# A one-core kernel of sparse attention and a gated feed-forward: keys of units 3 to 5 copied ahead of the first value gathers, and one weight piece loaded from another queue

## The chip, the core and the metric

One NeuronCore of one Trainium2 chip runs the whole program: TensorE (PE) for matmuls and transposes, VectorE (DVE), ScalarE (ACT), GpSimd (POOL) and SyncE (SP), with 16 DMA engines that serve the queues of SP, ACT and POOL. The metric is the device time of one launch in microseconds (us).

## What is computed

Block-sparse attention over 4 batches, 8 heads, 768 positions of width 64, then a feed-forward layer on the result. Cut to what matters:

```python
scores = scale * np.matmul(q, k.transpose(0, 1, 3, 2))
# kept: the diagonal block and its neighbours, the first and last block rows and columns,
# and three sampled key blocks for each block of queries (blocks of 32 positions)
attn = softmax(np.where(mask, scores, -1e9))
x = np.matmul(attn, v)              # laid out as 3072 tokens of 512
h = x @ w_in                        # 512 x 2048
sp = np.maximum(h, 0.0) + np.log1p(np.exp(-np.abs(h)))
out = (h * erf(sp)) @ w_out         # 2048 x 512
```

The two weights arrive as 64-bit floats, so each is 8.4 MB.

## The kernel before

**Units.** A batch has 24 blocks of 32 queries. The 22 inner blocks are worked on two at a time: unit n of a batch is blocks 1+2n and 2+2n, so there are 11 "m" units, and four "f" units more for the first and last block, which look at every key. For an m unit `scores` multiplies the queries (`qm`) with neighbouring keys, with the first and last block, and with the sampled keys; `soft_max`, `soft_exp` and `soft_turn` make probabilities (`less`, `pf`, and `pT`, the transposed and split copy); `values` multiplies them with the values into `po`; `norm` divides (`rinv`, `xf`); `turn` writes the transposed result to `xT`, from which the feed-forward starts. Four units make one chunk of `xT`.

**Sampled keys and values.** Which blocks are sampled is known only at run time. `gather` has POOL copy six key blocks for a unit from `kx` to two of the six buffers `kg` (three units' worth). Values go through a table in device memory: `split_v` scales and splits them (`vn`), SP stores `vn` to `vtab` (four stores), and `gather_v` fills one of six buffers `vbuf` per query block: one or two loads by SP (neighbours, and the first and last block) and one indirect DMA by POOL (the sampled blocks). `gathers(most)` first issues all key copies that have a free `kg`, then up to `most` value gathers that have a free `vbuf`.

**Weights.** `load_w` brings the weights in pieces: the first weight ("i") in eight pieces of 1 MB on SP, the second ("o") in six of 1 MB (named here wo0, wo2, to wo10 by their first row block, loaded by ACT's queue) and in pieces 12 to 15 of 0.5 MB each, which land in buffers `raw` that belong to other stages at other times. `decode` turns a pair of 64-bit rows into 32-bit floats in three DVE steps: `room<-wo`, `room<-wo,room`, `wo<-wo,room`. The loads wo0 to wo6 overwrite places of w_in pieces that must be decoded first, and wo8 and wo10 the places of wo4 and wo6. `weights()` runs the decode, the squares for a scale (`sq`), the 16-bit high and low halves and the correction `rest`; `ratios()` needs all of them, and the first gate of the feed-forward needs `ratios()`.

**Order.** SP and POOL issue in the order of the program. PE, ACT and DVE are put in order by the compiler up to the fourth group of the feed-forward, and from there in the order of the program too. The engines run their rows strictly in order. The warm-up is the loop over `begun` from 0 to 5 (`FIRST`): for each unit `values` of the unit two before it, its scores and softmax, then `gathers()`, then three steps of `weights()`. All later work is the loop over the groups of the feed-forward, one unit in most steps.

**Waits in rows of the program order.** DMAHW0 to DMAHW7 are eight semaphores that the DMAs of SP and ACT take in turn; a DMA also waits until the one that had its semaphore before has landed. DMASW are those of POOL's DMAs.

Of the kernel before, what the change touches and what calls it, by code (L numbers as in the profile page):

```python
# [31 lines left out]
def sparse_attention_moe(ctx: ExitStack, tc: tile.TileContext, qT, kT, v, sampled, w_in, w_out, out):  # L32
# [39 lines left out]
    KGS, VGS = 6, 6  # L72
# [90 lines left out]
    def order_q(b, u):  # L163
        t, half = divmod(u, 2)
        qt = qts[b, t][:, :, half * 2 * BLOCK : (half + 1) * 2 * BLOCK].rearrange("p r (j c) -> p r j c", c=BLOCK)
        for a in range(2):
            place = qms[half][a * D : (a + 1) * D, :, :, a, :]
            if b == 0 and 0 < u <= FIRST:
                act.activation(place, qt[a * D : (a + 1) * D], AF.Copy, scale=D**-0.5)
            else:  # L170
                dve.tensor_scalar(place, qt[a * D : (a + 1) * D], D**-0.5, None, ALU.mult)
# [219 lines left out]
    def load_w(key, i):  # L391

        if key == "o" and i >= 12:
            tag, bufs = (("vraw", 1), ("xT", 3), ("xT", 3), ("x", 2))[i - 12]
            rows = w_out[i * P : (i + 1) * P].bitcast(I32)
            if tag == "x":
                parts = [mo.tile([P, 512], I32, tag=tag, name=f"raw_{i}_{u}", bufs=bufs) for u in range(2)]
            elif tag == "vraw":
                parts = [ld.tile([P, H // 2, KT * D], I32, tag=tag, name=f"raw_{i}", bufs=bufs).rearrange("p a b -> p (a b)")[:, :1024]]
            else:  # L400
                parts = [mo.tile([P, 1024], I32, tag=tag, name=f"raw_{i}", bufs=bufs)]
            c = 0
            for raw in parts:
                (sp if i == 15 else act).dma_start(raw, rows[:, c : c + raw.shape[1]])
                c += raw.shape[1]
            places[key, i] = parts
            return
        if key == "i":
            raw = slots(wi, 1 + 2 * i, 4) if i < 8 else slots(wo, 2 * i - 16, 4)
            part, kt = divmod(i // 2, NK)  # L410
            sp.dma_start(raw, w_in[kt * P : (kt + 1) * P, part * 1024 : (part + 1) * 1024].bitcast(I32))
        else:
            raw = slots(wo, 2 + 2 * i if i < 8 else 10 + 2 * (i - 8), 4)
            rows = w_out[i * P : (i + 2) * P, :].bitcast(I32).rearrange("(n p) c -> p n c", n=2)
            act.dma_start(raw.rearrange("p (n c) -> p n c", n=2), rows)
        places[key, i] = [raw]
# [254 lines left out]
    def norm(b, u, part):  # L671
        po = pos.pop((b, u, part))
        tag = f"{b}_{u}_{part}"
        gr = slice(0, 4) if part is None else slice(2 * part, 2 * part + 2)
        n = gr.stop - gr.start
        rinv = st.tile([P, 4], F32, tag="rinv", name=f"rinv_{tag}")[:, :n]
        dve.tensor_scalar(rinv, po[:, gr, D], EPS * 2.0**P_SHIFT, None, ALU.add)
        dve.reciprocal(rinv, rinv)
        if not part:
            xfs[b, u] = at.tile([P, 4, D], F32, tag="xf", name=f"xf_{b}_{u}", bufs=1)  # L680
        dve.tensor_tensor(xfs[b, u][:, gr], po[:, gr, :D], rinv.unsqueeze(2).to_broadcast([P, n, D]), ALU.mult)
# [115 lines left out]
    units = []  # L797
# [9 lines left out]
    def gathers(most=VGS):  # L807

        nonlocal kfree, vfree
        while kjobs and kfree >= 2 and kjobs[0][0] in have_k:  # L810
            kfree -= 2
            gather(*kjobs.pop(0))
        while vjobs and vfree and most and vjobs[0][0] in have_v:
            gather_v(*vjobs.pop(0))
            vfree -= 1
            most -= 1
# [46 lines left out]
    def seen(unit):  # L863

        if unit[0] == "m":
            return unit[1], unit[2], None
        if unit[2] % 2 == 1:
            return unit[1], NU, unit[2] // 2
        return None
# [6 lines left out]
    def used_values(place):  # L876
        nonlocal vfree
        if place[2] is None:
            vfree += 2
        elif place[2] == 1:  # L880
            vfree += 3
# [19 lines left out]
    for i in range(0, 16, 2):  # L901
        if i in (0, 2, 6):
            load_q(0, 1 + (i + 1) // 3)
        if i:
            load_w("i", i)
    load_w("o", 15)
    order_q(0, 0)
    have_k.add(0)
    ixgen = indices()
    next(ixgen)  # L910
    gathers()
    with tc.high_priority():
        max_v(0, 0)
        max_v(0, 1)
# [5 lines left out]
            for half in range(2):  # L920
                split_v(0, quad, half)
    have_v.add(0)
    for i in (13, 12, 14):
        load_w("o", i)
    for begun in range(FIRST):
        with tc.high_priority():
            if begun >= 2:
                place = seen(units[begun - 2])
                values(*place)
                used_values(place)  # L930
                norm(*place)
                turn(*place, True)
            unit = units[begun]
            scores(unit)
            used_keys(unit)
            soft_max(unit)
            next_queries(begun)
            soft_exp(unit, True)
            soft_turn(unit)
        gathers()  # L940
        later(3)
        if 0 < begun < B:
            zero_rows(begun)
        if begun < 4:
            behind(begun)
# [106 lines left out]
```

## Time and profile before

| | us |
|---|---|
| median of 3 runs | 788.03 (783.29 to 788.62) |
| the profiled execution | 781.89 |
| its span on the core | 780.1 |
| PE busy | 716.6 (92%) |
| ACT busy | 597.8 (77%) |
| DVE busy | 556.1 (71%) |
| POOL busy | 201.4 (26%) |

The page's second part cuts the span into 40 slices of 19.5 us. PE is 2 to 7 tenths busy in the first four and 8 or 9 in all but the last. DMA is at 9 tenths in the first three slices. All that follows concerns the first 130 us; rows of the trace give the start of a group of instructions, its duration, its engine, the line (L48 is a helper that issues every operation, so tiles tell them apart), the operation, and in brackets the idle time just before it and what ended it. "SPq", "ACTq" are the queues' own DMA issues.

### The profile page before, as it was taken

How to read it: one execution, taken by the hardware profiler on the slowest of the kernel's cores; microseconds unless marked ns; L12 is line 12 of the kernel's file. 1: busy time of each engine (PE TensorE's matmuls, PEld its weight loads, DVE VectorE, ACT ScalarE, POOL GpSimd, SP SyncE). 2: the span in 40 equal slices, each digit the busy share in tenths (PEclk: the TensorE clock that was granted, in tenths of full speed). 3: DMA queues.
4: the chain of work that ended last, by engine and by line, in shares of the span. 5: the costliest groups of instructions: out<-in, count | busy, mean ns of one | idle time of the engine just before them, and what ended most of it. 6: DMA issues, size and time to landing. Idle time of an engine off the chain costs nothing.

```text
span 780.1 us, 26222 instructions
## 1 busy us (share of the span) xinstructions
PE 716.6 (92%) x11136; PEld 501.0 (64%) x11136; DVE 556.1 (71%) x1043; ACT 597.8 (77%) x1035; POOL 201.4 (26%) x397
## 2 busy tenths in 40 slices
PE   2447788999899999999999999999999999999997
PEld 1334546766577777666677776666767676666663
DVE  7795998887677777767766777757867766564553
ACT  3656799888768878888788777878778877787774
POOL 2247531314343312032423312033433120000000
PEclk9668999999999999999999999999999999999999
DMA  9999765997799986836989989828977676231000
GB/s 311 410 253 303 211 140 121 186 240 163 162 210 168 220 196 171 205 97 146 195 175 186 171 191 206 204 59 176 218 150 176 130 148 144 53 51 28 8 28 27
DMA packets 188053, 129.45 MB, mean 166 GB/s; under 512 B 137760, under 2 KB 160928, under 8 KB 186912
## 3 DMA queue, kind: packets, MB, share of 16 engines
q1 hardware_dynamic: 173440, 83.98, 51.7%
q10 hardware_dynamic: 8608, 25.96, 10.6%
q0 software_dynamic: 5888, 17.84, 9.7%
q8 instruction: 87, 1.43, 0.8%
q14 instruction: 30, 0.25, 0.1%
HBM read 82.81 MB, written 12.95 MB: 123 GB/s over the span
## 4 chain that ended last, share of the span: by engine, by line
PE 80%; DVE 7%; DMA 6%; ACT 3%; issue 2%; SPq 1%; ACTq 1%
PE h L48 31%; PE o L48 30%; PE s_m L48 9%; PE po_None L48 5%; PE s_f L48 2%; DMA qt<-in_qT_dram 2%; DMA wo<-in_w_out_dram 2%; DVE room L48 2%; PE po L48 1%; DVE wo L48 1%; ACT x L48 1%; DMA vbuf<-in_v_dram 1%; DMA pT_f<-p_f 1%; PE rest L48 1%; SPq L48 1%
## 5 line engine op out<-in xcount | busy, mean ns | idle before, releaser
L48 PE MATMUL h<-xT,wi 128*128 128x256 f16 x2304 | 272.1, 275 | 6.4 <-DVE y L48 4.5
L48 PE MATMUL o<-wo,g 128*128 128x512 f16 x1152 | 264.5, 379 | 0.3 <-DVE g L48 0.2
L48 PEld LDWEIGHTS <-wi 128*128 128x128 f16 x2304 | 223.6, 99 | 47.1 <-issue 4.8
L48 ACT ACTIVATE x<-x 128x512 f32<-128x512 f32 x288 | 181.3, 630 | 8.9
L48 PEld LDWEIGHTS <-g 128*128 128x128 f16 x1152 | 109.6, 98 | 120.4 <-DVE g L48 1.3
L48 POOL DMA_INDIRECT vbuf<-vtab,idx x88 | 103.5, 1176 | 250.2 <-PE po_None L48 170.6
L48 DVE SCALAR_TENSOR_TENSOR y<-y,x 128x512 f32<-128x512 f32 x96 | 66.2, 689 | 78.5 <-ACT x L48 78.5
L48 PE MATMUL s_m<-kx,qm 128*64 128x64 f32 (+1 forms) x1408 | 95.7, 247 | 26.6 <-DVE qm L48 14.3
L48 ACT ACTIVATE x<-h,isg 128x512 f32<-128x512 f32 x96 | 65.4, 681 | 69.0 <-PE h L48 67.3
L48 PEld LDWEIGHTS s_m<-kx,qm 128*64 128x64 f32 x1408 | 70.8, 145 | 36.2 <-ACT sq_i L48 14.3
L48 POOL COPY kg<-kx 128x128 f32 x264 | 79.7, 349 | 51.9 <-PE s_m L48 34.0
L48 ACT ACTIVATE y<-y 128x512 f32<-128x512 f32 x96 | 59.6, 621 | 35.2 <-DVE y L48 26.0
L48 DVE TENSOR_REDUCE less_m<-s_m 128x4 f32<-128x1024 f32 x44 | 53.7, 1221 | 35.2 <-PE s_m L48 35.2
L48 DVE SCALAR_TENSOR_TENSOR g<-y,sums,g 128x512 f16<-128x512 f32 x96 | 72.5, 756 | 3.4
L48 ACT ACTIVATE pf_m<-s_m,less_m 128x256 f32<-128x256 f32 x176 | 68.5, 472 | 4.6 <-PE turned L48 2.3
L48 PE MATMUL s_m<-kg,qm 128*64 128x96 f32 x704 | 65.4, 258 | 1.9 <-POOL kg L48 1.9
L48 DVE SCALAR_TENSOR_TENSOR y<-y,h 128x512 f32<-128x512 f32 x96 | 65.4, 681 | 0.7
L48 ACT ACTIVATE y<-x 128x512 f32<-128x512 f32 x96 | 60.4, 629 | 2.9
L48 PEld LDWEIGHTS <-pT_m 128*32 128x32 f16 x4224 | 38.6, 94 | 24.8 <-issue 20.1
L48 DVE TENSOR_SCALAR g<-y,sums 128x512 f16<-128x512 f32 x96 | 48.3, 504 | 3.4
L48 PE MATMUL po_None<-vbuf,pT_m 128*32 128x65 f16 (+1 forms) x4224 | 44.8, 196 | 3.9 <-ACT pf_m L48 2.9
L48 PEld LDWEIGHTS s_m<-kg,qm 128*64 128x64 f32 x704 | 45.2, 146 | 3.7 <-POOL kg L48 2.3
(106 smaller groups left out, 608.5 us busy)
## 6 DMA issues: line engine op xcount, KB each, us to landing
vbuf<-vtab SPq DMA_DIRECT2D x80, 195.0 KB
vraw<-in_v_dram ACTq DMA_DIRECT2D x9, 768.0 KB
vtab<-vn SPq DMA_DIRECT2D x16, 390.0 KB
vbuf<-vtab SPq DMA_DIRECT2D x12, 520.0 KB
wo<-in_w_out_dram ACTq DMA_DIRECT2D x6, 1024.0 KB
qt<-in_qT_dram SPq DMA_DIRECT2D x20, 256.0 KB
kr<-in_kT_dram ACTq DMA_DIRECT2D x12, 384.0 KB
vbuf<-vtab SPq DMA_DIRECT2D x32, 130.0 KB
```

The lines of the kernel that those rows point to most:

```text
L48: done = call(*args, **kwargs)
```

## The change

Piece 13 of the second weight is issued by SP right behind piece 15, where ACT issued it before, ahead of pieces 12 and 14. The first two units' calls of `gathers` now copy keys only (`gathers(0)`), and value gathers begin after unit 2; so POOL copies the keys of units 3, 4 and 5 before the first six value gathers. `values` of unit 0 moves from ahead of unit 2's scores to behind that round of gathers.

```diff
-                (sp if i == 15 else act).dma_start(raw, rows[:, c : c + raw.shape[1]])
+                (sp if i in (13, 15) else act).dma_start(raw, rows[:, c : c + raw.shape[1]])
...
     load_w("o", 15)
+    load_w("o", 13)
...
-    gathers()
+    gathers(0)
...
-    for i in (13, 12, 14):
+    for i in (12, 14):
         load_w("o", i)
     for begun in range(FIRST):
         with tc.high_priority():
-            if begun >= 2:
+            if begun >= 3:
                 place = seen(units[begun - 2])
                 values(*place)
...
-        gathers()
+        gathers(VGS if begun >= 2 else 0)
+        if begun == 2:
+            with tc.high_priority():
+                place = seen(units[0])
+                values(*place)
+                used_values(place)
+                norm(*place)
+                turn(*place, True)
```

The compiler's order moves with it. **Place 1.** ACT, early in the program, before: `raw_303` is piece 13, `qm` the scaled queries, `pf_m_0` the exponentials of unit 0.

```order
L48 ACTIVATE sq_i_401,sums<-wi 128x1024 [waits DMAHW2_49,DVE_49]
L48 ACTIVATE qm_111<-qt_0_133 64x8x32 [waits DMAHW6_49]
L48 ACTIVATE qm_111<-qt_0_133 64x8x32
L48 DMA raw_303<-in_w_out_dram 128x1024 [waits DMAHW0_49]
L48 ACTIVATE qm_110<-qt_1_146 64x8x32 [waits DMAHW4_49,DVE_49,PE_49]
L48 ACTIVATE qm_110<-qt_1_146 64x8x32 [waits DVE_49]
L48 ACTIVATE pf_m_0_338<-s_m_0_309,less_m_0_334 128x256 [waits DVE_49]
```

The same place of the changed program:

```order
L48 ACTIVATE sq_i_382,sums<-wi 128x1024 [waits DMAHW2_49,DVE_49]
L48 ACTIVATE qm_111<-qt_0_133 64x8x32 [waits DMAHW6_49]
L48 ACTIVATE qm_111<-qt_0_133 64x8x32
L48 ACTIVATE qm_110<-qt_1_146 64x8x32 [waits DMAHW4_49,DVE_49,PE_49]
L48 ACTIVATE qm_110<-qt_1_146 64x8x32 [waits DVE_49]
L48 ACTIVATE pf_m_0_338<-s_m_0_309,less_m_0_334 128x256 [waits DVE_49]
L48 ACTIVATE pf_m_0_338<-s_m_0_309,less_m_0_334 128x256 x3
L48 ACTIVATE pT_m_0_343<-turned 128x2x256 [waits PE_49,Activation_49]
```

The DMA that waited for DMAHW0 no longer stands between the queries of units 1 and 2; on SP it stands behind piece 15 and ahead of the first store to `vtab`.

**Place 2.** POOL, before, between the keys of unit 3 (`kg_8`) and those of unit 4 (`kg_9`, `kg_10`):

```order
L48 COPY kg_8_375<-kx_135 128x128 [waits PE_49,Pool_49]
...
L48 DMA vbuf_104<-vtab_115,idx 96x1040 [waits DMAHW2_49,DMAHW1_49,DMAHW3_49,DMASW1_49,DMAHW5_49,DMASW0_49,DVE_49]
L48 DMA vbuf_105<-vtab_115,idx 96x1040
...
L48 DMA vbuf_109<-vtab_115,idx 96x1040
...
L48 COPY kg_9_475<-kx_135 128x128 [waits PE_49,Pool_49]
...
L48 COPY kg_10_479<-kx_135 128x128 [waits PE_49,Pool_49]
```

and in the changed program, from the same row on:

```order
L48 COPY kg_8_375<-kx_135 128x128 [waits PE_49,Pool_49]
...
L48 COPY kg_9_456<-kx_135 128x128 [waits PE_49,Pool_49]
...
L48 COPY kg_10_460<-kx_135 128x128 [waits PE_49,Pool_49]
...
L48 COPY kg_11_562<-kx_135 128x128 [waits PE_49,Pool_49]
...
L48 COPY kg_12_566<-kx_135 128x128 [waits PE_49,Pool_49]
...
L48 DMA vbuf_104<-vtab_115,idx 96x1040 [waits DMAHW2_49,DMAHW1_49,DMAHW3_49,DMASW1_49,DMAHW5_49,DMASW0_49,DVE_49]
```

Twelve copies (two units) moved ahead of the six gathers, which wait for the stores to `vtab`.

**Place 3.** DVE, before, from the first decode step of wo4 (it waits for DMAHW4) to that of wo6 (DMAHW6), `rinv_1` being the norm of unit 1:

```order
L48 TENSOR_SCALAR room<-wo 128x1024 [waits DMAHW4_49]
L48 SCALAR_TENSOR_TENSOR room<-wo,room 128x1024 [waits DVE_49]
L48 TENSOR_SCALAR rinv_1_None<-po_1_None 128x4 [waits PE_49]
L48 SCALAR_TENSOR_TENSOR wo<-wo,room 128x1024 [waits DVE_49]
L48 RECIPROCAL rinv_1_None<-rinv_1_None 128x4 [waits DVE_49]
L48 TENSOR_SCALAR sums<-allm_wi_736 128x1 [waits PE_49]
L48 TENSOR_SCALAR room<-wo 128x1024 [waits DMAHW6_49]
```

and in the changed program, wo4 by DMAHW6 and wo6 by DMAHW7:

```order
L48 TENSOR_SCALAR room<-wo 128x1024 [waits DMAHW6_49]
L48 TENSOR_SCALAR rinv_1_None<-po_1_None 128x4 [waits PE_49]
L48 TENSOR_REDUCE less_m_5_1384<-s_m_5_1359 128x4 [waits PE_49]
L48 TENSOR_SCALAR qm_111<-qt_3_152 64x8x32 x2
L48 SCALAR_TENSOR_TENSOR room<-wo,room 128x1024 [waits DVE_49]
L48 RECIPROCAL rinv_1_None<-rinv_1_None 128x4 [waits DVE_49]
L48 TENSOR_SCALAR sums<-allm_wi_732 128x1 [waits PE_49]
L48 TENSOR_SCALAR room<-wo 128x1024 [waits DMAHW7_49]
L48 SCALAR_TENSOR_TENSOR wo<-wo,room 128x1024 [waits DVE_49]
```

The last decode step of wo4, which frees the place of wo8, now stands behind the row that waits for wo6, and its second step behind the norm of unit 1 and the maximum of unit 5.

## Rows read from the trace of the kernel before

**Rows 1.** Windows: us, busy us (x instructions) per engine, granted clock, DMA share, GB/s.

```profile
86.00:128.00 42.00, 32.95 (x516) 22.64 (x517) 38.83 (x91) 38.39 (x72) 12.20 (x22) 0.92 0.59 136
128.00:200.00 72.00, 72.00 (x1185) 50.27 (x1184) 57.28 (x107) 62.26 (x107) 16.46 (x31) 0.98 0.86 181
200.00:780.00 580.00, 569.02 (x8792) 396.82 (x8790) 394.65 (x715) 448.68 (x764) 131.09 (x264) 1.00 0.69 144
```

**Rows 2.** Windows again, same columns, cut where the DMA load changes.

```profile
45.00:53.25 8.25, 3.82 (x50) 3.67 (x50) 8.25 (x11) 5.09 (x11) 3.89 (x1) 0.71 0.68 182
53.25:90.00 36.75, 26.69 (x488) 16.69 (x490) 25.89 (x49) 24.43 (x51) 28.32 (x47) 0.83 1.03 308
90.00:96.00 6.00, 6.00 (x108) 4.28 (x106) 6.00 (x13) 4.94 (x9) 0.51 (x1) 0.96 0.03 10
```

**Rows 3.** Timeline of DVE: its waits for softmax, weight pieces and queries.

```profile
28.02 0.69 DVE L48 SCALAR_TENSOR_TENSOR pT_m<-turned,pT_m 128x512 f16<-128x512 f32 x1 [3.70 <-ACT pT_m L48]
...
57.23 0.69 DVE L48 TENSOR_SCALAR room<-wo 128x1024 int32<-128x1024 int32 x1 [1.28 <-DMA wo<-in_w_out_dram]
...
64.75 0.75 DVE L48 TENSOR_SCALAR room<-wo 128x1024 int32<-128x1024 int32 x1 [4.30 <-DMA wo<-in_w_out_dram]
...
71.98 0.90 DVE L48 TENSOR_SCALAR room<-wo 128x1024 int32<-128x1024 int32 x1 [2.10 <-DMA wo<-in_w_out_dram]
...
74.46 1.21 DVE L48 SCALAR_TENSOR_TENSOR wo<-wo,room 128x1024 int32<-128x1024 int32 x1
...
78.40 0.69 DVE L48 TENSOR_SCALAR room<-wo 128x1024 int32<-128x1024 int32 x1 [1.39 <-DMA wo<-in_w_out_dram]
...
86.07 0.73 DVE L48 TENSOR_SCALAR room<-wo 128x1024 int32<-128x1024 int32 x1 [1.02 <-DMA wo<-in_w_out_dram]
...
101.06 0.59 DVE L48 TENSOR_SCALAR qm<-qt 64x256 f32<-64x256 f32 x2 [0.75 <-DMA qt<-in_qT_dram]
```

**Rows 4.** Timeline of ACT: piece 13, what follows it, and loads of wo.

```profile
24.27 0.38 ACTq L48 DMA_DIRECT2D raw<-in_w_out_dram  x1
24.78 0.85 ACT L48 ACTIVATE qm<-qt 64x256 f32<-64x256 f32 x2 [9.87 <-DVE i_v L48]
...
50.53 0.41 ACTq L48 DMA_DIRECT2D wo<-in_w_out_dram  x1
...
59.74 1.48 ACT L48 ACTIVATE wi<-wi,sums 128x512 f16<-128x512 f32 x2 [2.75 <-DMA vbuf<-vtab]
...
76.86 0.38 ACTq L48 DMA_DIRECT2D wo<-in_w_out_dram  x1
```

**Rows 5.** Chain that ended last, in order of time: start, us, what.

```profile
14.16 10.09 DMA qt<-in_qT_dram
24.27 0.38 ACTq L48
24.78 0.42 ACT qm L48
```

**Rows 6.** Timeline of POOL: key copies and the first value gather.

```profile
17.55 1.48 POOL L48 COPY kg<-kx 128x128 f32 x6 [0.69 <-issue]
...
20.84 3.98 POOL L48 COPY kg<-kx 128x128 f32 x6 [0.38 <-PE allm_v L48]
49.13 3.89 POOL L48 DMA_INDIRECT vbuf<-vtab,idx  x1 [24.31 <-DMA vtab<-vn]
...
61.24 1.47 POOL L48 COPY kg<-kx 128x128 f32 x6
```

**Rows 7.** Timeline of PE: scores of unit 4, values of units 0 and 1.

```profile
62.05 0.38 PE L48 MATMUL s_m<-kg,qm 128*64 128x96 f32 x2 [1.87 <-POOL kg L48]
...
67.40 0.95 PE L48 MATMUL po_None<-vbuf,pT_m 128*32 128x65 f16 x95
...
70.79 0.96 PE L48 MATMUL po_None<-vbuf,pT_m 128*32 128x65 f16 x96
```

**Rows 8.** Timeline of SP's DMA issues: piece 15, stores to vtab, value loads.

```profile
20.92 2.95 SPq L48 DMA_DIRECT2D raw<-in_w_out_dram  x2
31.71 9.33 SPq L48 DMA_DIRECT2D vtab<-vn  x4
48.42 47.52 SPq L48 DMA_DIRECT2D vbuf<-vtab  x21
```

## The prediction

> **What bounds the kernel now.** I read the windows first, then the waits of each engine in the first 130 us, then the program's order. From 128 us on PE is the bound: busy 72.00 of 72.00 us up to 200, 569.02 of 580.00 after [rows 1]. The change touches nothing there, because the rows from the fourth feed-forward group on keep the order of the program; so its worth is the time by which that stretch begins earlier or later. Before it, PE is not the bound. In 86 to 128 us DVE is busy 38.83 of 42.00 us and ACT 38.39 [rows 1], with the decode of the last weight pieces, their halves and the softmax of units 3 to 7, all of it ahead of the first gate. What starts that stretch is the landing of wo8 at 86.07 [rows 3]. And what sets that landing is the DMA stage ahead of it: from 53.25 to 90 us the DMA engines are loaded 1.03 with 308 GB/s, and in the same time DVE stands five times waiting for a piece of wo, at 57.23, 64.75, 71.98, 78.40 and 86.07, 10.1 us in all [rows 2, 3]. So the question is whether wo8 lands earlier.
>
> Just ahead of that stage there is a gap: from 45 to 53.25 us the DMA moves only 182 GB/s [rows 2]. Nothing is queued: wo0 is issued at 50.53 [rows 4], since its place must be decoded first, and DVE, busy 8.25 of 8.25 us there [rows 2], gets to it no sooner.
>
> **Part 1, piece 13 leaves ACT's queue (place 1).** Its DMA waits for DMAHW0, on which queries landed at 14.16 + 10.09 = 24.25 [rows 5]; it is issued at 24.27, and ACT has by then been idle 9.87 us, from 14.9 [rows 4]. (The idle row names DVE; the chain names the transfer, and the next row of ACT waits only for queries and a free buffer.) Behind it stand the queries of unit 2, the exponentials of unit 0, then its transposes; DVE, free at 24.32, waits 3.70 us for the second half of that work, to 28.02 [rows 3]. Without the DMA ACT can go on at about 20, when unit 0's maximum is there, and DVE has no wait at 24.32, if the weight piece it decodes next has landed; that piece was queued ahead of the queries that landed at 24.25 [rows 5], so it has. DVE's stream up to the decode that frees wo0 is busy, so it moves by the whole 3.7 us, and wo0 is issued at about 47 where it was 50.53.
>
> What is that worth at the DMA? The gap is short of the stage's rate by (308 - 182) x 8.25 = 1.04 MB, or 3.4 us at 308 GB/s [rows 2]. That is the upper bound. The lower is nothing: the value gathers cannot start before the stores to `vtab` have landed (48.42 [rows 8]), and those are bytes that queue behind all of w_in as before. The loads come 3.5 us earlier in a gap of 8.25, so I take half: **-1.7 us** (0 to -3.4).
>
> The piece on SP costs SP nothing that is wanted: it waits there for the same landing, to 24.25, and SP's next row is a store to `vtab`, issued at 31.71 [rows 8], 28 if DVE is 3.7 earlier. Its 0.5 MB now lie ahead of the stores in SP's own queue and no longer in ACT's; all must be moved ahead of the gathers either way, so 0. If they did delay the stores it would be 0.5 MB / 308 GB/s = 1.7 us on the gathers.
>
> The Trainium skill ("DMA: Bandwidth & Descriptors", "Issuing engines are not separate DMA queues") says that all queues end in the same 16 DMA engines and that issuing from another one saves only the issuing engine's time. By that rule the move is worth the 0.38 us of the issue. The rows agree on the bytes, but not on the size of what the issuing engine loses: 9.87 us of waiting.
>
> **Part 2, keys ahead of gathers (place 2).** Six copies take 1.47 us [rows 6]. Before, POOL stood 24.31 us waiting for `vtab` with unit 4's copies behind it, and copied them at 61.24; PE, at the scores of unit 4, waited 1.87 us for them, and the values of unit 0 stood behind those scores, running at 67.40 [rows 6, 7]. Now both units' copies lie in POOL's idle time (12 copies, 2.9 us, or 8.0 by the slowest row, 3.98 for six, where POOL has 24.31 idle [rows 6]); they wait for the scores of units 1 and 2, which PE has done by then. So the scores, the maximum and the exponentials of unit 4 move out of the way, and the values of unit 0 can run when their gathers land. I estimate 65, from 67.40. But all of this lies beside the DMA stage: DVE's rows for it fill its 10.1 us of waits. Worth on the path: 0.
>
> The copies now run beside DVE. In the row of 3.98 us they were slowed to 0.66 us each, against 0.25 for the row of 1.48 [rows 6]. It was POOL that waited, and POOL has time; cost 0. The Trainium skill ("SBUF — State Buffer", "SBUF: two separate sides") says that GpSimd and a DVE instruction with two inputs in that memory exclude each other for a whole instruction, whichever comes first. If DVE always lost, 12 copies of 0.25 would cost it up to 3 us; nothing in the rows shows DVE losing.
>
> **Part 3, what the compiler's order does to wo8 (place 3).** Before, the last decode step of wo4 ran at 74.46, its place was free at 75.67, and wo8 was issued at 76.86, before wo6 landed at 78.40; so ACT's queue went from wo6 to wo8 without a break and wo8 landed 86.07 - 78.40 = 7.67 us after wo6 [rows 3, 4]. Now that step stands behind the row that waits for wo6: 0.69 + 1.21 us after its landing [rows 3] the place is free, and wo8 can be issued 2.0 us after wo6 landed. From then it starts on an empty queue. The nearest row is wo0, which did so: issued 50.53 [rows 4], landed 57.23 [rows 3], 6.7 us. So wo8 lands 8.7 us after wo6 and not 7.67: **+1.0 us**. Bounds: 1.05 MB at the full 308 GB/s is 3.4 us, so 5.4 after wo6 (-2.3); or as slow as before, 7.67, so 9.7 (+2.0).
>
> **Part 4, after wo8.** DVE's wait of 0.75 us at 101.06 is for queries that SP issues behind the value loads of unit 6, which wait for the values of unit 3 [rows 3, 8]. The rows that these values need stand a little nearer to wo8 in DVE's new order, so I take the wait as gone: **-0.75** (0 to -0.75).
>
> **Sum:** -1.7 + 1.0 - 0.75 = -1.45 us. Against the profiled execution's own 781.89 that gives 780.4. The timed runs lie higher, 783.29 to 788.62 with a mean of 786.6 and a median of 788.03, so as a median of runs I say 786.6 - 1.45, near **785**.
>
> **Rivals.** *Nothing gained.* The gap at 45 to 53 is not filled because the gathers come late by what wo0 comes early, and wo8 keeps its distance to 128 us: 786.6. For it: the stage is bound by bytes, and no byte is saved. Against: in the gap the load was 0.68 [rows 2].
>
> *More gained.* The whole gap is filled (-3.4) and, the gathers being through, wo8 moves alone (-2.3, and -0.75): -6.5 us, 780. For it: DMA load falls to 0.03 at 90 us [rows 2], so a queue does empty. Against: both bounds would have to hold at once.
>
> *Slower: DVE's order ties the weights to the values.* The second decode step of wo4 now stands behind the norm of unit 1 and the maximum of unit 5 (place 3), that is behind PE's values of unit 1. These ended at 71.75 and wo4 landed at 71.98 [rows 7, 3], a tie. If they are later than wo4, wo4, wo8 and all behind it are late by the difference. Price: if piece 13 and piece 14 (issued earlier by ACT now) delay the stores, 2 x 1.7 = 3.4, and with +1.0 from part 3 it is +4.4, or 791. It decides as soon as the values of unit 1 end after wo4's landing. For it: values wait for gathers, gathers for stores. Against: the values of unit 0 lose their wait behind unit 4's scores.
>
> **How the numbers follow.** Chances: forecast 0.5, nothing gained 0.2, more gained 0.15, slower 0.15. A measurement of this kernel can tell about 1% (7.9 us) from no change; each case's centre is within that, and only scatter of the runs, some 3 us either way, and cases beyond their bounds carry it out: faster by over 1% 0.1, slower 0.06, within 0.84. The range is 780 (all that can be gained) to 791 (the slower rival).
>
> **What would show it.** Right: no idle of 9.87 us on ACT; DVE's pT step at 24.3; wo0 issued near 47; key copies of units 4 and 5 before 48; wo8 issued about 2 us after wo6 lands and landing near 85; PE's steady stretch from about 126.5. Wrong: `vtab` landing well after 50, values of unit 1 after 73, or wo0 still issued near 50.

## The result, and the profile after

The changed kernel is slower by about one per cent: a median of 796.44 us over 6 runs (794.05 to 801.28) against 786.79 for the kernel before in the same measurement, a ratio of 1.0107 (95% interval 1.0068 to 1.0146). A second measurement, 12 runs against 35, gave 1.0049 (1.0019 to 1.0079), 790.15 against 786.00. So there is a loss, by the medians of 4.2 us in one measurement and 9.7 in the other. The forecast was 785, with a range of 780 to 791.

| | before | after | before, 2nd trace | after, 2nd trace |
|---|---|---|---|---|
| the profiled execution, us | 781.89 | 794.05 | 786.22 | 793.94 |
| its span | 780.1 | 792.3 | 784.4 | 792.2 |
| steady stretch of PE begins at | 127.85 | 134.06 | 130.61 | 133.21 |

"Steady stretch" here and below is the first group of `h` matmuls that PE starts after a wait for DVE's `y`; from there the feed-forward runs at PE's pace. The first trace of before is one of its shortest executions; in a second one the same kernel begins the stretch 2.8 us later. Comparing the means (133.6 and 129.2), the warm-up lost about 4.4 us. The spans differ by more, 10.0 us in the mean (792.25 and 782.25). So the other 5.6 us lie behind the start of the steady stretch, where the forecast expected no change. Some 3.6 of them lie in one place, shown under "What stays open". The text up to there is about the warm-up.

Windows of after, with the columns of [rows 1, 2] (us, busy us and instructions of PE, PEld, DVE, ACT and POOL, granted clock, DMA share, GB/s):

```profile
0.00:45.00 45.00, 16.63 (x200) 14.41 (x202) 38.64 (x87) 24.32 (x47) 21.52 (x50) 0.83 0.98 348
45.00:53.25 8.25, 3.04 (x34) 2.69 (x32) 8.25 (x12) 6.03 (x13) 2.50 (x2) 0.71 1.03 287
53.25:90.00 36.75, 23.76 (x451) 16.21 (x448) 20.41 (x39) 18.74 (x39) 20.34 (x33) 0.77 0.91 257
128.00:200.00 72.00, 62.69 (x942) 43.25 (x943) 57.13 (x108) 58.88 (x101) 15.88 (x25) 0.91 0.94 177
200.00:780.00 580.00, 573.32 (x9002) 401.82 (x9001) 397.46 (x715) 455.71 (x776) 132.09 (x274) 1.00 0.70 145
```

There is a gain and then a larger loss. The gap at 45 to 53.25 us is filled: 287 GB/s where it was 182. Then 53.25 to 90 runs at 257 GB/s where it was 308 [rows 2]. That is (308 - 257) x 36.75 = 1.9 MB less moved, against (287 - 182) x 8.25 = 0.9 MB more in the gap. DVE is busy 20.41 us of that stretch and was 25.89. From 128 to 200 us PE is busy 62.69 and was 72.00 [rows 1]; 6.06 us of the difference is the wait before 134.06.

What is missing from the DMA engines are the loads of wo4 and wo6. Timeline of ACT in after (start, duration, engine, operation, in brackets the idle time and what ended it):

```profile
18.46 0.85 ACT L48 ACTIVATE qm<-qt 64x256 f32<-64x256 f32 x2 [3.37 <-PE s_m L48]
...
47.27 0.39 ACTq L48 DMA_DIRECT2D wo<-in_w_out_dram  x1
...
66.88 1.18 ACTq L48 DMA_DIRECT2D wo<-in_w_out_dram  x2
68.19 1.06 ACT L48 ACTIVATE sq_o<-wo 128x1024 bf16<-128x1024 f32 x1 [13.28 <-DMA vbuf<-vtab]
...
83.20 0.38 ACTq L48 DMA_DIRECT2D wo<-in_w_out_dram  x1
```

and the chain that ended last, in the same place:

```profile
52.51 14.35 DMA vbuf<-vtab
66.86 0.02 issue
66.88 0.38 ACTq L48
```

wo0 is issued at 47.27 instead of 50.53, as planned. But wo4 and wo6, which ACT had issued before it went on at 59.74 [rows 4], now go out at 66.88, because a value load, issued at 52.51, lands at 66.86. They stand in ACT's queue, and ACT stands behind them, idle for 13.28 us. The wait is for a semaphore, not for the data: of the eight that the DMAs of SP and ACT take in turn, wo4's was last used by that value load. In the order of before the load eight DMAs ahead of wo4 was an earlier one (the rows of the second value buffer, where it is now those of the third), since the new order puts the two loads of the last value buffer ahead of wo4. In before it is wo6 that waits for the third buffer's rows. There they were issued at 51.08 and let wo6 go at 59.26, so in after the load itself is also later.

DVE then waits for the pieces:

```profile
60.09 0.69 DVE L48 TENSOR_SCALAR room<-wo 128x1024 int32<-128x1024 int32 x1 [3.06 <-DMA wo<-in_w_out_dram]
...
76.63 0.69 DVE L48 TENSOR_SCALAR room<-wo 128x1024 int32<-128x1024 int32 x1 [9.40 <-DMA wo<-in_w_out_dram]
...
88.76 0.76 DVE L48 TENSOR_SCALAR room<-wo 128x1024 int32<-128x1024 int32 x1 [0.83 <-DMA wo<-in_w_out_dram]
...
95.43 0.69 DVE L48 TENSOR_SCALAR room<-wo 128x1024 int32<-128x1024 int32 x1 [2.23 <-DMA wo<-in_w_out_dram]
```

These are wo2, wo4, wo8 and wo10. wo4's wait is 9.40 us long; before, wo4 was ready at 71.98 after 2.10 [rows 3]. wo8 comes at 88.76 instead of 86.07.

The queues between 56 and 68 us, after (packets, MB, share of the 16 engines; q10 is ACT's, q1 SP's, q0 POOL's):

```profile
q1 hardware_dynamic: 947, 1.63, 58.9%
q0 software_dynamic: 427, 1.18, 41.3%
q10 hardware_dynamic: 22, 0.07, 2.5%
```

and before:

```profile
q10 hardware_dynamic: 462, 1.80, 51.4%
q0 software_dynamic: 359, 1.17, 33.9%
q1 hardware_dynamic: 347, 0.59, 17.7%
```

ACT's queue carried 1.80 MB of weights there and now carries 0.07. The value loads have taken part of its place: the stretch moves 240 GB/s where it moved 298.

This was the first reading: ACT is held, the weights are late, the warm-up ends late. The experiments show that only a part of it is true.

### The profile page after: what moved, and what is told of

It is laid out like the page before. It is cut to its first block, busy times and chain, and to the rows that moved or that the text cites. A ratio compares the mean times of both kernels' runs of the same rounds, so it can differ in the third digit from the quotient of the medians.

```text
span 792.3 us, 26235 instructions
## 1 busy us (share of the span) xinstructions
PE 721.8 (91%) x11136; PEld 505.0 (64%) x11136; DVE 559.2 (71%) x1043; ACT 597.9 (75%) x1035; POOL 202.5 (26%) x397
## 4 chain that ended last, share of the span: by engine, by line
PE 66%; DVE 10%; DMA 10%; ACT 7%; issue 4%; SPq 1%; ACTq 1%; POOL 0%; another core or an unknown queue 0%; POOLq 0%; DVEq 0%
PE h L48 26%; PE o L48 25%; PE s_m L48 8%; PE po_None L48 4%; DMA vtab<-vn 4%; ACT x L48 2%; DMA vbuf<-vtab 2%; DVE room L48 2%; PE s_f L48 1%; DVE wo L48 1%; DMA qt<-in_qT_dram 1%; DMA wo<-in_w_out_dram 1%; DVE y L48 1%; DVE vn L48 1%; SPq L48 1%
## 5 line engine op out<-in xcount | busy, mean ns | idle before, releaser
L48 POOL DMA_INDIRECT vbuf<-vtab,idx x88 | 99.3, 1128 | 243.3 <-PE po_None L48 183.2
L48 PE MATMUL s_m<-kx,qm 128*64 128x64 f32 (+1 forms) x1408 | 98.6, 251 | 32.2 <-ACT pf_m L48 16.3
L48 POOL COPY kg<-kx 128x128 f32 x264 | 85.2, 368 | 65.6 <-PE s_m L48 44.3
L48 PEld LDWEIGHTS s_m<-kx,qm 128*64 128x64 f32 x1408 | 72.8, 148 | 43.5 <-ACT pf_m L48 17.7
L48 DVE SCALAR_TENSOR_TENSOR p_m<-pf_m,p_m 128x1024 f16<-128x1024 f32 x38 | 46.3, 1218 | 0.2 <-ACT p_m L48 0.2
```

The costliest lines, as they stand in the source:

```text
L48: done = call(*args, **kwargs)
```

## The experiments

All ratios are against the kernel before, timed beside it on the same chip, 12 runs of each edit, with the 95% interval. Two numbers of each trace are followed: when wo10's decode starts on DVE, and when the steady stretch begins.

### Each part alone

Piece 13 alone:

```diff
-                (sp if i == 15 else act).dma_start(raw, rows[:, c : c + raw.shape[1]])
+                (sp if i in (13, 15) else act).dma_start(raw, rows[:, c : c + raw.shape[1]])
...
     load_w("o", 15)
+    load_w("o", 13)
...
-    for i in (13, 12, 14):
+    for i in (12, 14):
```

> The kernel before with one part of the change: the 13th piece loaded by SyncE. The loads of wo4 and wo6 still wait for the loads of buffer 105's rows and buffer 106's rows, as before. Theory A (the loss is ACT held at the loads of wo4 and wo6, because the order made by the keys part lets them wait for buffer 106's loads): no loss here, 784 to 788 us, ratio 0.996 to 1.002; wo0 issued at 47 to 49; ACT held 2 to 6 us at wo6, not 13. Theory B (the earlier loads of wo0 and wo2 slow the value loads down, whatever the order): buffer 106's rows land at 64 or later here too, ACT held some 8 us, 791 to 796 us.

Measured: 0.9981 (0.9953 to 1.0008), 787.08 against 788.75. Its ACT:

```profile
61.57 5.36 ACTq L48 DMA_DIRECT2D wo<-in_w_out_dram  x2
67.03 1.48 ACT L48 ACTIVATE wi<-wi,sums 128x512 f16<-128x512 f32 x2 [13.33 <-DMA vbuf<-vtab]
```

ACT is held 13.33 us here too, as long as in after, and wo4 is decoded only at 75.37. Yet the steady stretch begins at 129.84 and the time is that of before or a little less. So neither ACT's wait nor a late wo4 is by itself the loss; neither theory above fits whole, since the first had no long hold and the second had 791 to 796 us with one. The piece's own worth, -1.5 us, is near Part 1's -1.7, but the interval holds zero.

The other part alone, keys ahead and the values of unit 0 moved, with piece 13 left to ACT:

```diff
-    gathers()
+    gathers(0)
...
-            if begun >= 2:
+            if begun >= 3:
...
-        gathers()
+        gathers(VGS if begun >= 2 else 0)
+        if begun == 2:
+            with tc.high_priority():
+                place = seen(units[0])
+                values(*place)
+                used_values(place)
+                norm(*place)
+                turn(*place, True)
```

> The kernel before with the other part alone: keys of units 3 to 5 and values of unit 0 in the new order; the 13th piece stays on ACT. The load of wo4 then waits for buffer 106's rows and wo6 for buffer 106's ends, with wo0 and wo2 issued near 50.5 and 51.7 as before. Theory A: ACT is held at wo4 from about 57 until buffer 106's rows land, 5 to 10 us more than the 2.75 of before; 790 to 797 us, ratio 1.004 to 1.013. Theory B: value loads as in before, buffer 106's rows landing near 59, ACT held about 3 us; 786 to 788 us.

Measured: 1.0068 (1.0040 to 1.0097), 794.77 against 788.75. A loss of the size of after's is in this part. The traced execution, 788.56, is one of its two shortest, 6.2 us under the median, so the trace does not show all that the typical run loses. Its DVE:

```profile
73.29 0.70 DVE L48 TENSOR_SCALAR room<-wo 128x1024 int32<-128x1024 int32 x1 [0.96 <-DMA wo<-in_w_out_dram]
...
75.93 0.16 DVE L48 TENSOR_SCALAR rinv_None<-po_None 128x4 f32<-128x4 f32 x1 [1.94 <-PE po_None L48]
...
78.19 1.24 DVE L48 SCALAR_TENSOR_TENSOR room<-wo,room 128x1024 int32<-128x1024 int32 x1
```

ACT is held only 3.36 us here and wo4 lands by 73.29, but its second decode step stands behind the norm of unit 1, which waits for PE's values, and runs at 78.19. That is the mechanism of the slower rival, seen as it was described. The end is the same as in after: wo10 at 94.95, steady at 133.59. Two different waits, then, with one end; the question becomes what comes behind wo10.

The keys part was then cut in two, roughly: the keys of unit 5 ahead of the gathers are in neither half. Keys of units 3 and 4 ahead of the gathers, the values of unit 0 left where they were:

```diff
     for begun in range(FIRST):
+        if begun == 2:
+            gathers()
...
-        gathers()
+        gathers(VGS if begun >= 2 else 0)
```

> The kernel before with GpSimd's order alone: the keys of units 3 and 4 are copied ahead of the first gathers of values, while the values, norm and turn of unit 0 keep their place in the program. Theory D1 (the loss comes from where GpSimd and SyncE put the gathers and value loads): 790 to 797 us, ratio 1.004 to 1.012. Theory D2 (it comes from writing unit 0's values behind unit 2's scores, which re-orders DVE, ACT and PE from 50 to 130 us): 785 to 790 us, ratio 0.997 to 1.002.

Measured: 1.0004 (0.9974 to 1.0034). And the values of unit 0 written behind unit 2's scores, with the gathers as before:

```diff
-            if begun >= 2:
+            if begun >= 3:
...
+        if begun == 2:
+            with tc.high_priority():
+                place = seen(units[0])
+                values(*place)
...
```

> The kernel before with the other half of the keys part alone: GpSimd's gathers where they were, but unit 0's values, norm and turn written behind unit 2's scores, softmax and the gathers. Theory D2: 790 to 797 us, ratio 1.004 to 1.012, the last loads of the second weight decoded at 95 or later, DVE idle more than 12 us in all between 55 and 100. Theory D1: 785 to 790 us.

Measured: 1.0018 (0.9986 to 1.0050). Neither half costs anything that can be told from nothing; both of them together do, though the intervals of the second half and of the whole overlap (up to 1.0050, and from 1.0040). In both traces wo10 is decoded late, at 97.34 and 97.91, and the steady stretch still begins at 131.17 and 132.60, 33.8 and 34.7 us behind it, where the kernel with both halves needs 38.6. So it is the stretch behind wo10 that tells them from the whole. The start itself tells less: the second half's is only 1.0 us ahead of the whole's.

### Both kernels once more

> The changed kernel once more, for a second trace and for a time beside the parts: 793 to 799 us, ratio 1.007 to 1.014. If its trace shows ACT held at the loads of wo4 and wo6 for much more or less than 13 us at the same total, that wait does not set the time.

> The kernel before once more, for a second trace: 784 to 791 us, ratio 0.997 to 1.003. What is open is how much the landing of buffer 106's rows (59.26 us in the first trace) and the first steady group of h (127.85 us) move from one execution to the next: under 1 us if the traces stand for the kernel, several us if the transfers of this stretch fall out differently each time.

Measured: 1.0049 (1.0019 to 1.0079) and 0.9995 (0.9962 to 1.0028). The 793 to 799 us expected of after did not come (790.15). The second trace of before shows how far its own warm-up moves:

```profile
59.24 6.35 ACTq L48 DMA_DIRECT2D wo<-in_w_out_dram  x2
65.69 1.48 ACT L48 ACTIVATE wi<-wi,sums 128x512 f16<-128x512 f32 x2 [8.38 <-DMA vbuf<-vtab]
...
96.14 0.69 DVE L48 TENSOR_SCALAR room<-wo 128x1024 int32<-128x1024 int32 x1 [1.31 <-DMA wo<-in_w_out_dram]
```

It is the same program, and ACT goes on 6 us later, at 65.69 where it was 59.74 [rows 4], held 8.38 us where it was 2.75; and wo10 is decoded at 96.14 where the first trace has 92.51. That is no earlier than in after (95.43 and 94.82). Yet before begins its steady stretch at 130.61 and after at 134.06 and 133.21. So against this trace the warm-up's loss lies wholly behind wo10.

What lies there is DVE's work. Windows from the start of wo10's decode to the start of the steady stretch (columns as above; DVE is the third pair), first before and before a second time:

```profile
92.51:127.85 35.34, 27.53 (x413) 18.53 (x412) 32.24 (x78) 32.71 (x61) 11.01 (x18) 0.95 0.58 122
```

```profile
96.14:130.61 34.47, 24.90 (x358) 17.55 (x357) 31.95 (x77) 31.11 (x58) 11.23 (x18) 0.94 0.56 135
```

piece 13 alone:

```profile
94.82:129.84 35.02, 27.42 (x412) 18.64 (x412) 32.27 (x77) 32.56 (x61) 10.80 (x18) 0.95 0.55 123
```

after, after a second time, and the keys part alone:

```profile
95.43:134.06 38.63, 29.15 (x384) 19.34 (x383) 35.16 (x85) 34.19 (x63) 11.85 (x18) 0.85 0.55 122
```

```profile
94.82:133.21 38.39, 27.16 (x364) 18.42 (x364) 34.99 (x85) 32.77 (x61) 10.53 (x16) 0.85 0.46 116
```

```profile
94.95:133.59 38.64, 28.15 (x381) 19.63 (x380) 35.15 (x85) 33.67 (x63) 10.93 (x18) 0.87 0.47 121
```

In all six DVE is busy but for 2.5 to 3.5 us (35.34 - 32.24 = 3.1 in before, 38.63 - 35.16 = 3.5 in after). So in these six the stretch is as long as DVE's work in it, plus some 3 us, and the keys part leaves DVE 85 instructions and 35.1 us of work there instead of 78 and 32.1. Counted row by row, the seven more are two first steps of decoding pieces 12 and 13 (`room<-raw`), a transposed block (`xT`), three small scale rows (`sums`), and one `y<-y,x` of the second gate.

The first of these show where they came from. Order of DVE before (two rows of pieces 12 and 13, and behind them wo10's first step, which waits for a DMA):

```
L48 TENSOR_SCALAR room<-raw_305 128x512 [waits DVE_49]
L48 TENSOR_SCALAR room<-raw_303 128x512
L48 SCALAR_TENSOR_TENSOR xT_0_621<-turned,xT_0_621 128x2x128 [waits Activation_49]
L48 SCALAR_TENSOR_TENSOR pT_m_4_1147<-turned,pT_m_4_1147 128x2x256 [waits Activation_49]
L48 TENSOR_SCALAR room<-wo 128x1024 [waits DMAHW7_49]
```

and after:

```
L48 TENSOR_SCALAR room<-wo 128x1024 [waits DMAHW6_49]
L48 SCALAR_TENSOR_TENSOR xT_0_691<-turned,xT_0_691 128x2x128 [waits Activation_49]
L48 TENSOR_SCALAR sums<-total_945 128x1 [waits PE_49]
L48 TENSOR_SCALAR room<-raw_305 128x512 [waits DVE_49]
L48 TENSOR_SCALAR room<-raw_163 128x512
```

The decode of pieces that have long landed moved from ahead of a row that waits for the last weight to behind it. DVE waits at that row (2.23 us in after) with the work in its hands queued behind it. From the start to wo10, in before and in after:

```profile
0.00:92.51 92.51, 47.90 (x748) 35.22 (x749) 71.80 (x147) 54.02 (x106) 42.89 (x84) 0.82 0.95 309
0.00:95.43 95.43, 48.77 (x778) 37.48 (x779) 70.51 (x139) 52.60 (x104) 44.92 (x85) 0.78 0.94 300
```

Of the 2.9 us more behind wo10, 1.3 were ahead of it before (DVE is busy 71.80 us up to there in before, 70.51 in after). The rest, 1.6, is work that before does behind the first gate: DVE's work up to the steady stretch is 71.80 + 32.24 = 104.0 in before and 70.51 + 35.16 = 105.7 in after.

### Undoing what holds the weights

On after, the short loads (first and last block) of all six value buffers ahead of their long ones:

```diff
-            if ends_of.get(n) != b:
-                ends_of[n] = b
+            for e in range(VGS) if turn_of[0] == 1 else (n,):
+                if ends_of.get(e) != b:
+                    ends_of[e] = b
...
-                sp.dma_start(vg[NR * BLOCK :], ends)
+                    sp.dma_start(vbufs[e][NR * BLOCK :], ends)
```

> The changed kernel with SyncE's first value loads in another order: the ends (32x2x1040) of all six buffers ahead of the 96-row loads of buffers 105 to 109; the same bytes. Eight DMAs ahead of wo4 then stands the ends of buffer 107 and ahead of wo6 those of buffer 108, which land early. Theory A: ACT's idle of 13.28 us at that place falls under 4 us, wo4 is issued by 58, its transfer lands by 72, wo8 lands near 85, and the time comes back to 784 to 789 us. Theory C (the loss is the new order on DVE around the decode of wo4 and wo6, or late value loads as such): ACT's idle moves and 792 to 797 us stay.

Measured: 0.9994 (0.9968 to 1.0019). The time is that of before, but the trace, of an execution of 791.76 among runs of 783.72 to 795.90, shows ACT idle 13.90 us and the steady stretch at 135.91. It does not show why the median came back. I draw nothing from it.

On after, wo4 and wo6 issued by SP, behind the loads of all six value buffers, so that ACT can't be held:

```diff
-            act.dma_start(raw.rearrange("p (n c) -> p n c", n=2), rows)
+            (sp if i in (4, 6) else act).dma_start(raw.rearrange("p (n c) -> p n c", n=2), rows)
```

> The changed kernel with the loads of wo4 and wo6 issued by SyncE behind the six value loads, in place of ACT: they still wait for buffer 106's loads and start no earlier than about 66, but ACT no longer stands behind that wait. If the loss is the work held on ACT (scores of unit 5, halves of wi): 785 to 790 us, with the scores of unit 5 back near 65 and the values of unit 1 back near 71. If it is the weights that come late: wo4 lands at 75 or later as in the changed kernel, wo8 and wo10 are late as well, and 792 to 797 us stay.

Measured: 1.0041 (1.0014 to 1.0068). ACT is free, and the weights are not earlier:

```profile
64.57 1.82 SPq L48 DMA_DIRECT2D wo<-in_w_out_dram  x2
```

```profile
75.41 0.78 DVE L48 TENSOR_SCALAR room<-wo 128x1024 int32<-128x1024 int32 x1 [10.45 <-DMA wo<-in_w_out_dram]
```

wo10 follows at 95.10, DVE has 35.08 us of work behind it, and PE is steady at 134.15. Freeing the engine that issues is worth nothing that can be told here (1.0041, where after had 1.0049 and 1.0107). The Trainium skill ("DMA: Bandwidth & Descriptors", "Issuing engines are not separate DMA queues") says as much: issuing from another engine saves only the time of its sequencer. This run agrees with it. What the move could have changed, and this one did not, is the place among the other loads.

The next runs change that place. On after, wo4 and wo6 by SP behind four value buffers:

```diff
-        gathers(VGS if begun >= 2 else 0)
+        gathers(VGS if begun > 2 else 4 if begun == 2 else 0)
...
         later(3)
+        if begun == 2:
+            gathers()
```

> The changed kernel with the loads of wo4 and wo6 issued by SyncE ahead of the value loads of buffers 108 and 109, in place of ACT behind all six buffers; they then wait for no load of buffer 106, and ACT does not stand behind them. Theory E (the loss is the weights wo4 to wo10 coming late, behind value loads that land at 65 to 67, so that DVE waits for them and starves ACT): wo4 lands before 70, DVE's wait for it falls from 9 to 11 us to under 4, the first steady group of h starts before 131 (133.21 and 134.06 in the two traces of the changed kernel), 783 to 788 us. Theory F (the new order on the engines behind 95 us costs 3 us whenever the weights come): the first steady h at 131 or later and 787 to 792 us.

Measured: 0.9996 (0.9967 to 1.0024).

```profile
72.26 0.69 DVE L48 TENSOR_SCALAR room<-wo 128x1024 int32<-128x1024 int32 x1 [6.71 <-DMA wo<-in_w_out_dram]
```

And behind two (the 4 above is a 2):

> As e7_after_wo4_first, but wo4 and wo6 already ahead of the values of buffer 106 (only buffers 104 and 105 ahead of them). In e7 SyncE issued them at 60.6, wo4 was decoded at 72.26, DVE had waited 6.71 us for it, and the first steady group of h came at 128.69. Theory E (the later the weights, the later the steady state): issued by 57, decoded by 68, DVE's wait under 3 us, first steady h at 125 to 128, 781 to 786 us and not slower than e7. Against it: the values of units 1 and 2 now come 3 to 5 us later (unit 1's were at 68 to 71.5 in e7), and if PE's order then waits for them the time stays at 785 to 790 us.

Measured: 0.9963 (0.9927 to 0.9999), 782.04 against 785.66. This is the only version here whose interval lies below one, and barely; among so many versions that is weak evidence of a gain over before. Against after, whose intervals lie above one, it is clearly better.

```profile
53.57 5.43 SPq L48 DMA_DIRECT2D wo<-in_w_out_dram  x2
```

```profile
69.26 0.69 DVE L48 TENSOR_SCALAR room<-wo 128x1024 int32<-128x1024 int32 x1 [0.73 <-DMA wo<-in_w_out_dram]
```

```profile
92.00:126.19 34.19, 28.07 (x410) 19.64 (x397) 30.25 (x75) 31.84 (x62) 11.47 (x18) 1.00 0.56 132
```

All three kernels have the keys part and piece 13 on SP; only the place of two loads differs:

| wo4 and wo6 stand behind | wo4 decoded at | DVE's wait for it | wo10 decoded at | DVE's work behind wo10 | steady at | ratio |
|---|---|---|---|---|---|---|
| six value buffers | 75.41 | 10.45 | 95.10 | 35.08 | 134.15 | 1.0041 |
| four | 72.26 | 6.71 | 93.16 | 31.32 | 128.69 | 0.9996 |
| two | 69.26 | 0.73 | 92.00 | 30.25 | 126.19 | 0.9963 |

The earlier the two loads, the shorter the wait and the sooner the steady stretch: 8 us between first and last, of which 3 are wo10's and 5 are DVE's work behind it. The two go together in these runs, since the compiler puts DVE's rows in another order in each kernel, and the runs do not separate them. The spans of the first and the last differ by the same 8.0 us (788.5 and 780.5). The middle one's does not follow: at 787.6 it gives back 4.6 us behind the start of the steady stretch, for a reason that is not known.

### The same place without the keys ahead

If the place of wo4 is what counts, before should gain from it as well. On before, first with piece 13 on SP, then without:

```diff
-            act.dma_start(raw.rearrange("p (n c) -> p n c", n=2), rows)
+            (sp if i in (4, 6) else act).dma_start(raw.rearrange("p (n c) -> p n c", n=2), rows)
...
-        gathers()
+        gathers((4, 0, 0)[begun] if begun < 3 else VGS)
         later(3)
+        if begun == 2:
+            gathers()
```

> The kernel before with the 13th piece on SyncE (as in the change), the first value gathers cut to four buffers, and wo4 and wo6 loaded by SyncE between the values of buffers 107 and 108. Keys and unit 0's values keep their place in the program. Theory E: DVE's 3.7 us earlier start of the piece is kept, since the weights come by 70; first steady h at 124 to 127, 779 to 784 us, faster than the kernel before. If the transfers as a whole set the stretch (the same bytes in another order): first steady h near 130, 785 to 789 us.

> As the run before it, but with the 13th piece on ACT as in the kernel before: only the order of value loads and weights differs from the kernel before. Theory E: wo4 lands by 70 in place of 72 to 74, 783 to 787 us; the difference to the run before it is what the 13th piece on SyncE is worth once the weights are in time, 2 to 4 us by theory E, nothing if the transfers set the stretch.

Measured: 1.0018 (0.9994 to 1.0043) and 1.0060 (1.0030 to 1.0090). Before gains nothing; the 779 to 784 expected of the first and the 783 to 787 of the second did not come, and the second is slower than before. In both traces a wait appears on PE that the kernels with the keys ahead do not have; of the second:

```profile
61.25 0.58 PE L48 MATMUL s_m<-kg,qm 128*64 128x96 f32 x2 [5.39 <-POOL kg L48]
```

The keys of unit 4 are copied behind the gathers, and PE waits 5.39 us for them (1.87 in before, [rows 7]). wo10's decode is early in the first (92.39), but the steady stretch only comes at 131.47, 39.08 us behind it; in the second at 133.82, 38.77 behind. The window of the first:

```profile
92.39:131.47 39.08, 28.38 (x367) 18.74 (x366) 32.86 (x81) 33.17 (x63) 7.76 (x16) 0.87 0.45 107
```

DVE's work is 32.86 us of the 39.08 here, and 32.83 of 38.77 in the second. So in these two DVE is idle for some 6 us behind wo10, and the length of its work is not the whole account. That speaks for the keys ahead: they remove a wait that counts once the weights are in time. The ratios alone do not prove it (1.0018 here, 0.9996 for the same place with the keys ahead; the intervals overlap). Between the medians of this pair stand 2.7 us, the worth of piece 13 there. It has the sign of the first experiment's -1.5, though neither pair of intervals is narrow enough to fix it; and with the keys ahead the piece shows no gain (after's 1.0049 and 1.0107, the keys part alone 1.0068).

## Why the prediction was wrong, step by step

**The step that failed** is Part 2's "Worth on the path: 0". The keys part alone measured 1.0068 (1.0040 to 1.0097), 6 us by the medians, against a forecast of -1.45 us for the whole change. What the runs showed in its place: the part puts the value loads of all six buffers ahead of wo4 and wo6, and in its new order DVE has 35.1 us of work behind wo10 where it had 32.1. With the same keys part (and piece 13 on SP), but the two loads issued ahead of the last four buffers' values, the ratio is 0.9963. Why DVE's order leaves it more work behind wo10 is not shown.

**What bounds the kernel.** Right for a part: the steady stretch came some 4 us later, and the time with it. But "The change touches nothing there" is not what the traces show, since 5.6 us of the 10.0 between the spans lie behind its start. Two more things were missing. The profiled execution was taken as typical apart from its level, when in it the value load that held ACT had landed early (ACT went on at 59.74, and at 65.69 in the second trace). And wo8's landing was taken as what sets the end. In the traces the work that DVE has left when the last piece comes counts as well: in before's second trace wo8 and wo10 are decoded as late as in after (88.20 and 96.14 against 88.76 and 95.43), and its steady stretch still begins 3 us sooner.

**Part 1, piece 13.** Its first half came true: ACT's wait of 9.87 us [rows 4] is gone (`qm` at 18.46), the transposed step of unit 0 runs at 24.39 without a wait, DVE has done 38.64 us of work by 45 us where it had 35.15, and wo0 is issued at 47.27 (forecast 47). The gap was filled. What failed here is the sentence "The loads come 3.5 us earlier": it carries wo0's gain over to all the loads behind it. wo0 and wo2 do come earlier. wo4 and wo6 do not depend on DVE's decode alone; they wait for a value load, and the new order hung wo4 on one that lands at 66.86. The sign of it was on record: the wait of 2.75 us that ends with `vbuf<-vtab`, in [rows 4], is a weight load waiting in ACT's queue for a value load. It was shown and not priced. Piece 13 alone still measured -1.5 us, but with wo4 decoded at 75.37, later than before; so where the number is near the forecast, it is luck as far as these runs show.

**Part 2, keys ahead.** The copies cost nothing that shows. POOL's copies, beside DVE, took

```profile
21.14 8.95 POOL L48 COPY kg<-kx 128x128 f32 x12 [0.47 <-PE allm_v L48]
...
37.23 4.80 POOL L48 COPY kg<-kx 128x128 f32 x6 [6.01 <-PE s_m L48]
```

0.75 and 0.80 us each, where six had taken 1.48 [rows 6], and they were done by 42, ahead of the gathers. DVE did not lose in that time: the same decode step takes as long beside the copies (after) as with POOL idle (before).

```profile
25.80 1.23 DVE L48 SCALAR_TENSOR_TENSOR room<-wi,room 128x1024 int32<-128x1024 int32 x1
29.35 1.23 DVE L48 SCALAR_TENSOR_TENSOR room<-wi,room 128x1024 int32<-128x1024 int32 x1
```

The rule of the Trainium skill ("SBUF — State Buffer", "SBUF: two separate sides") that the two exclude each other, whichever starts first, fits if DVE is mostly first; the up to 3 us for DVE that it allowed did not come. An estimate that failed here is the values of unit 0 "at 65, from 67.40" with all behind it hidden in DVE's waits: unit 0's ran at 64.80, but unit 1's at 75.31 (70.79 before, [rows 7]), past the 73 named as the sign against the forecast. And "Worth on the path: 0" left out that the part moves the value loads of all six buffers, and its scores and norms, ahead of wo4 and of the decode.

**Part 3, wo8's place.** Forecast: wo8 lands 8.7 us after wo6, near 85. It is issued 2.1 us behind wo6's decode start at 81.07 (83.20), as worked out, and landed by 88.76, 7.7 us after it, as far as in before: the term came to nothing where +1.0 was taken, within its bounds. It was the base, wo6, that was late: 81.07 instead of 78.40 [rows 3] or less.

**Part 4, the wait for queries.** Gone as forecast; its worth is too small to be told from the rest.

**The slower rival** had the right sign and came nearest (791, where 796.44 and 790.15 were measured), with a chance of 0.15. Its mechanism, wo4's decode tied to the values of unit 1, shows in the keys part alone (78.19). In after it had little part to play: the values of unit 1 ran at 75.31, ahead of wo4 at 76.63, so the weight itself was as late as the tie. What it did not have is the order behind wo10, where the compiler left DVE 3 us more to do.

**What stays open.** The order behind wo10 was counted in six traces, not changed by itself: moving the decode of pieces 12 and 13 ahead of wo10 was not tried. Both traces of after also lose time later, in a wait for `vraw` and then for `y`. Of the first:

```profile
193.15 1.12 ACT L48 ACTIVATE vn<-vraw,s_v 128x384 f16<-128x384 f32 x2 [2.79 <-DMA vraw<-in_v_dram]
...
196.47 4.45 PE L48 MATMUL h<-xT,wi 128*128 128x256 f16 x24 [2.88 <-DVE y L48]
```

The next 24 `h` matmuls, at 206.02, took 2.79 us and not 4.45. The same 96 `h` matmuls and what stands between them, in before and in after, and then 3 us of after behind the wait:

```profile
167.20:194.30 27.10, 27.10 (x402) 18.06 (x398) 21.19 (x39) 23.19 (x38) 9.72 (x22) 1.00 0.91 193
174.20:206.00 31.80, 28.90 (x396) 18.91 (x395) 22.01 (x39) 24.94 (x41) 8.02 (x22) 0.95 0.90 172
197.00:200.00 3.00, 3.00 (x17) 2.13 (x15) 2.99 (x4) 2.06 (x4) 2.33 (x7) 0.51 0.57 180
```

So the wait of 2.88 us is followed by a fall of the granted clock to its lower level, 1.2 GHz (0.51 in the last window; 1.00 in before's), and the stretch is 4.7 us longer; in the second traces it is 31.60 in after and 29.05 in before. That is the larger part of what after loses behind the start of the steady stretch. The keys part alone and the kernel with wo4 on SP do not show this wait in their one trace each. The latter begins its steady stretch as late as after (134.15) and is 3.8 us shorter (788.5 against 792.3). So the wait comes on top of the warm-up's loss. How often it comes in the timed runs, and why the load lands late, I do not know. Nor is it known why the order of the short loads brought the median back.

## What to carry to other kernels

When a change moves DMAs, follow every later DMA that the same semaphores or the same queue tie to the moved ones; a small wait of a load for an unrelated load is where a larger one will stand. Where an in-order engine is almost saturated up to a deadline, count its work ahead of and behind the row that waits for the last input: in the traces of before and after, what an order left behind that row lengthened the stretch. When the time and one marker disagree, look behind the marker too. And take a second profile of the kernel before, if the forecast rests on when one transfer lands.

## What the runs showed of the hardware

The landing of one value load (the third buffer's rows) moves by 6 us between two executions of one program (ACT, which waits for it, goes on at 59.74 and at 65.69); the traces do not show me why, and the engine that issues the next load on its semaphore stands still until then (2.75, 8.38, 13.28 and 13.33 us in four traces). I had not expected that such a hold of ACT could cost nothing that can be told: at 13.33 us the kernel with piece 13 alone was as fast as before (0.9981, 0.9953 to 1.0008). Key copies on POOL took 0.75 to 0.80 us each beside a busy DVE, where others took 0.25, while a DVE step beside them took its 1.23 us as without them.
